# Eight blocks of tokens in a new order: the two-tile block of layer 1 second instead of last, with new scheduling priorities

## The chip, the cores and the metric

The kernel runs on one core of a Trainium2 chip. The metric is the device time of one execution in microseconds (us), lower is better. TensorE (PE) multiplies matrices, VectorE (DVE), ScalarE (ACT) and GpSimd (POOL) work elementwise, SyncE (SP) issues the transfers.

## The reference

Three stages follow each other. First an mLSTM over 768 steps, 4 batches and 8 heads of size 40, with a recurrent state `C`, a normalizer `n` and a running maximum `m`:

```
for t in range(S):
    m_new = np.maximum(f_gate[:, :, t] + m, i_gate[:, :, t])
    f_stab = np.exp(f_gate[:, :, t] + m - m_new)
    i_stab = np.exp(i_gate[:, :, t] - m_new)
    C = f_stab[:, :, None, None] * C + i_stab[:, :, None, None] * np.einsum('bhd,bhe->bhde', vt, kt)
    n = f_stab[:, :, None] * n + i_stab[:, :, None] * kt
    ...
    y[:, :, t] = o * h_tilde / denom
```

Its result, 3072 tokens of 320 features, goes through two layers of 320 to 2048 to 320. The first has a leaky ReLU, the second `h * cos(h)`:

```
h = x @ w_in
g = np.maximum(0.01 * h, h)      # layer 2: g = h * np.cos(h)
return g @ w_out
```

## The kernel before

The tokens are cut into 24 tiles of 128 (two batches by 64 steps). A tile of attention (called tile c below) is made in chunked form: scores of 64 by 64 per head (`a_scores`), weighted by products of the gates (`a_scan`, `a_weigh`), then `a_out` multiplies them with the values, reads the state of the tile two before and makes the state's increment. VectorE adds and normalizes (`a_ys`, `a_norm`, `a_scale`, `a_gate`), TensorE transposes the result (`x_turn`, L469), and ScalarE and VectorE split it into a high and a low part (`x_hi`, `x_lo`, L481 and L482). Two tiles of each 64 steps are independent; the next two need their states.

Each layer works in blocks of tiles (`BLOCKS1`, `BLOCKS2`), and each block in 16 slots, one for each 128 columns of the hidden width. In a slot `m_in` (L705) does eight matmuls of up to 512 columns, ScalarE and VectorE apply the nonlinearity and split its result (`m_leak` and `m_lo`; in layer 2 `m_turns`, `m_arg`, `m_cos`, `m_mul`, `m_hi`, `m_lo`), and `m_out` (L773) does three matmuls for each tile into banks that hold over all 16 slots. A block of layer 1 can start when the attention of all its tiles is done. A hidden tile of layer 1 has two banks of PSUM (ring `h`), but in the last block of layer 1 and in layer 2 there are four, since the attention's banks (`p`, `tr`) are then free.

The weights come as 64-bit floats. For each slot a weight is decoded (`w_bits` L386, `w_tail` L390, `w_sign` L394, `w_round` L398 on POOL, `w_mask` L402) and split into high and low (`w_hi` L201 or L199, `w_lo` L417). The sixteen weights of layer 1 are decoded beside the first tiles and block 0. Those of layer 2 are decoded during layer 1, stored, loaded again and split in the last block of layer 1, each when the weight in its buffer is no longer used. While TensorE has nothing else, `g_busy` (L251) keeps it at filler matmuls until the first slots.

What sets the order is a planner, `Schedule.run`, which runs when the kernel is built. Every piece of work is a task with a priority (a due time), a duration, the tasks that it needs, and the buffers that it takes and frees. The planner steps through a simulated time: of the tasks that could start soonest on an engine (within `SLACK`) it takes the one with the lowest priority number, and the instructions of each engine are issued in that order. On the chip each engine keeps this order and waits for semaphores. The due time of an attention tile is `t_need[c]`, that of a slot `t_slot`:

```
t_need[c] = t - ATT_LEAD - (m - 1 - j) * ATT_GAP if n else t - (m - 1 - j) * ATT_STEP
...
slot = max(slot, SLOT0)
...
p = t_slot[0, 0, i] - DEC_LEAD
plan_split(0, i, p + OFF["w_hi"], plan_decode(0, i, p))
```

and each step of a tile or slot stands at its due time minus or plus an offset in `OFF`. `T_START` is the planned time of the first slot, `SLOT0` the least planned length of a slot in block 0, `OUT_LAG` how far behind its slot an `m_out` stands.

Of the kernel before, what the change touches and what calls it, by code (L numbers as in the profile page):

```python
# [43 lines left out]
F32_MAX = float(np.finfo(np.float32).max)  # L44
STEEP = math.atanh(0.5) / (1.06 * 2.0 ** -15)

BLOCKS1 = [4, 3, 3, 3, 3, 3, 3, 2]
BLOCKS2 = [3] * 8
LAT = 0.204
SLACK = 0.05  # L50
SLOW = 50.0
T_START = 19.114
ATT_LEAD = 11.227
BACKLOG = 0.465
HORIZON = 180.0
ATT_GAP = 17.089
ATT_STEP = 8.185
OUT_LAG = 8.751
SLOT0 = 5.678
DEC_LEAD = 5.605  # L60
BUSY = [-1.11, 44.0, 0.7, -11.9]
SPREAD = 4
TURNS = [(0, 2), (2, 4), (4, 8), (8, 12)]
GATES_AT = 40.379
TURN_LEAD = 27.165
W2 = {0: -2.233, 1: -16.869}
OFF = {
    "fb": 109.16, "kvo": 6.159, "qk": 17.437, "vext": -8.48, "scan": 108.588, "kt": 17.196, "s": 16.51, "weigh": 96.927, "out": 14.378,
    "sig": 19.521, "ys": 107.91, "norm": -34.5, "scale": 120.878, "gate": 83.183, "state": 89.383, "decay": 60.278, "tr": 76.529,
    "x2": 15.514, "l_a": -93.128, "l_g": -74.411, "l_cos": 40.715, "l_mul": 46.316, "l_gh": 57.895,  # L70
    "l_gl": 97.565, "w_round": -23.988, "w_mask": 40.019, "w_hi": -83.534, "w_lo": 94.398, "w_load": 20.018,
}

ORDER = [(s, p) for s in range(NS) for p in range(B // 2)]
# [6 lines left out]
class Schedule:  # L81
# [13 lines left out]
    def run(self):  # L95
# [3 lines left out]
        while todo:  # L99
# [3 lines left out]
            for n, t in enumerate(todo):  # L103
                prio, _, key, alts, fn, args, deps, take, free, after, tab, size = t
                if prio > limit:
                    break
                ready = max(after, dma - BACKLOG) if size else after
                for d in deps:
# [19 lines left out]
            for eng, cs in cands.items():  # L128
                first = min(c[0] for c in cs)
                c = min((c for c in cs if c[0] <= first + SLACK), key=lambda c: c[1:])  # L130
                if len(todo[c[2]][3]) > 1:
# [4 lines left out]
                    if c[0] + c[3] > end + 1e-9:  # L136
# [3 lines left out]
                        first = min(x[0] for x in rest)  # L140
                        c = min((x for x in rest if x[0] <= first + SLACK), key=lambda x: x[1:])
                if best is None or (c[0], c[1]) < best[0]:
# [26 lines left out]
def mlstm_moe(ctx, tc, qk, kvo, ig, fg, w1, w2, const, out):  # L169
# [24 lines left out]
    sch = Schedule()  # L194
# [13 lines left out]
    def dvp(n):  # L208
        return ("DVE", 0.065 + n * 0.00105)
# [122 lines left out]
    def plan_gates():  # L332
# [11 lines left out]
        for j in range(2):  # L344
            sch.add(("eye", j), -4, ("POOL", 1.2, "port"), g_eye, j, deps=["cst"])
        for c0, c1, pr in ((0, 2, -3.0), (2, NS, GATES_AT)):
            n = (c1 - c0) * T
# [8 lines left out]
        for c0, c1 in TURNS:  # L356
            pr = {0: -3.0, 2: GATES_AT}.get(c0, t_need[BLOCKS1[0]] - TURN_LEAD)
            ring = "acc" if c0 < 4 else "tr"
# [6 lines left out]
            sch.add(("col", c0), pr + 0.7, dvp(48 * (c1 - c0)), g_input, c0, c1, deps=[("turn", c0)], free=[(ring, ("pt", c0))])  # L365
        sch.add("sf", GATES_AT + 0.5, SP, g_store, 2, NS, deps=[("cut", 2)], free=[("st", "f")], **dma(10 * T, BH))

# [72 lines left out]
    def plan_weights():  # L440
        for i in range(NF):
            p = t_slot[0, 0, i] - DEC_LEAD
            plan_split(0, i, p + OFF["w_hi"], plan_decode(0, i, p))
        n = len(BLOCKS1) - 1
        t0, t1 = t_slot[0, 2, 0] + W2[0], t_slot[0, n, 0] - W2[1]
        for i in range(NF):
# [46 lines left out]
    state = [cp.tile([P, 2 * HD, E1], F32, name=f"state{p}") for p in range(B // 2)]  # L493
# [69 lines left out]
    def po_ring(c):  # L563
        return "acc" if c < BLOCKS1[0] else "tr"

# [75 lines left out]
    def plan_attention(n, c, j, m):  # L641
        s, p = ORDER[c]
        e = t_need[c]
        last, k = s == NS - 1, (0, c)
        c0 = max(c for c, _ in TURNS if c <= s)
        for hh in range(2):
            sch.add(("qk", c, hh), e - OFF["qk"] + 0.1 * hh, SP, a_qk, c, hh, take=[] if hh else [("raw", c, 1)],
                    deps=[("qk", c, 0)] if hh else [], **dma(8 * P, DP))
        sch.add(("kvo", c), e - OFF["kvo"], SP, a_kvo, c, take=[("kvo", c, 2)], **dma(KV))
        if c < SPREAD:  # L650
            sch.add(("fb", c), e - OFF["scan"] - 2, ("PE", 1.0), a_spread, c, deps=[("cut", 0), "cst"],
                    take=[("acc", ("fp", c), 1), ("fb", c, 1)], free=[("st", "f")])
        else:
            for r in range(2):
                sch.add(("fb", c, r), e - OFF["fb"] + 0.1 * r, SP, a_fb, c, r, deps=[("fb", c, 0) if r else "sf"],
                        take=[] if r else [("fb", c, 1)], **dma(H * T, T))
        sch.add(("scan", c), e - OFF["scan"], ("DVE", 1.13) if c < SPREAD else ("DVE", 1.13, "port"), a_scan, c,
                deps=([("fb", c)] if c < SPREAD else [("fb", c, 0), ("fb", c, 1)]) + [("eye", 0), ("eye", 1)],
                free=[("acc", ("fp", c))] if c < SPREAD else [])
        sch.add(("vext", c), e - OFF["vext"], [pool(H * E1), dve(H * E1)], a_vext, c, deps=[("kvo", c), ("col", c0)])  # L660
        kt = []
        if not last:
            kt = [("kt", c)]
            sch.add(("kt", c), e - OFF["kt"], [pool(DM), dve(DM)], a_kt, c, deps=[("kvo", c), ("scan", c)])
        sch.add(("s", c), e - OFF["s"], ("PE", 0.62), a_scores, c, deps=[("qk", c, 0), ("qk", c, 1), ("scan", c), "clear"] + kt,
                take=[("p", (c, 0), (s > 0) + (not last)), ("p", (c, 1), (s > 0) + (not last))])
        sch.add(("weigh", c), e - OFF["weigh"], dvp(4 * P), a_weigh, c, deps=[("s", c), ("scan", c)] + kt)
        sch.add(("sig", c), e - OFF["sig"], ("ACT", 0.36), a_sig, c, deps=[("kvo", c), ("exp", 2, "f"), ("exp", 2, "i")], table="sig")
        sch.add(("out", c), e - OFF["out"], ("PE", 1.05 + (0.45 if s else 0) + (0.27 if not last else 0)), a_out, c,
                deps=[("weigh", c), ("vext", c)] + ([("state", c - 2)] if s else []) + kt  # L670
                + ([("col", TURNS[-1][0])] if c == BLOCKS1[0] else []),
                take=[(po_ring(c), ("po", c), 1)], free=[("fb", c), ("raw", c), ("kvo", c)])
        if s:
            sch.add(("ys", c), e - OFF["ys"], ("DVE", 0.82), a_ys, c, deps=[("out", c)], free=[("p", (c, 0)), ("p", (c, 1))])
        sch.add(("norm", c), e - OFF["norm"], ("DVE", 0.55), a_norm, c, deps=[("ys", c) if s else ("out", c)], take=[("d", c, 1)])
        sch.add(("scale", c), e - OFF["scale"], [pool(DM), dve(DM)], a_scale, c, deps=[("norm", c), ("sig", c)], free=[("d", c)])
        sch.add(("gate", c), e - OFF["gate"], dvp(DM), a_gate, c, deps=[("scale", c)], take=[("x", k, 1)],
                free=[(po_ring(c), ("po", c)), ("kvo", c)])
        if not last:
            if s:  # L680
                sch.add(("decay", c), t_need[c - 2] - OFF["decay"], [pool(H * E1), dve(H * E1)], a_decay, c, deps=[("state", c - 2), ("col", c0)],
                        take=[("tmp", c, 1)])
            sch.add(("state", c), e - OFF["state"], dvp(H * E1) if s else [("ACT", 0.35), dvp(H * E1)], a_state, c,
                    deps=[("out", c)] + ([("decay", c)] if s else []), free=[("p", (c, 0)), ("p", (c, 1))] + ([("tmp", c)] if s else []))
        plan_x(0, n, c, j, e - OFF["tr"], ("gate", c), ax, "x", m)
# [4 lines left out]
    def h_ring(l, n, i):  # L690
        return ("h", "h", "p", "tr")[i % 4] if l or n == len(BLOCKS1) - 1 else "h"

# [104 lines left out]
    def plan_layer(l, n, c0, m):  # L797
        N = m * P
        blocks = (BLOCKS1, BLOCKS2)[l]
        for i in range(NF):  # L800
# [24 lines left out]
            if l == 0 and last:  # L825
                free.append(("w", (0, i)))
            sch.add(("mo", k), p + OUT_LAG, ("PE", 3 * min(m, 3) * pe(1, DM)[1] + 6 * max(m - 3, 0) * pe(1, DM // 2)[1]), m_out, l, n, m, i, deps=[("gl", k)] + ([("mo", (l, n, i - 1))] if i else []),
                    take=take, free=free)
        for j in range(m):
            p = t_slot[l, n, NF - 1] + OUT_LAG + 1 + 0.3 * j  # L830
            sch.add(("ev", l, n, j), p, act(DM, True), m_evac, l, n, j, deps=[("mo", (l, n, NF - 1))],
# [8 lines left out]
    t_slot, t_need = {}, {}  # L840
    t, c = T_START, 0
    for l, blocks in enumerate((BLOCKS1, BLOCKS2)):
        c = 0
        for n, m in enumerate(blocks):
            slot = pe(8, m * P)[1] + pe(3 * m, DM)[1]
            if l == 0:
                for j in range(m):
                    t_need[c] = t - ATT_LEAD - (m - 1 - j) * ATT_GAP if n else t - (m - 1 - j) * ATT_STEP
                    c += 1
                slot += (2.8 * blocks[n + 1] / NF if n + 1 < len(blocks) else 0)  # L850
            if l == 0 and n == 0:
                slot = max(slot, SLOT0)
            for i in range(NF):
# [4 lines left out]
    c = 0  # L858
# [5 lines left out]
    c = 0  # L864
# [59 lines left out]
```

## Time and profile before

| | us |
|---|---|
| median of 3 runs | 839.64 (837.85 to 840.19) |
| the profiled execution | 839.06 |
| its span, first to last instruction | 837.3 |
| TensorE busy | 816.1 |
| VectorE busy | 593.2 |
| ScalarE busy | 421.3 |
| POOL busy | 123.9 |

The span is the stretch that the trace covers; the execution has 1.76 us outside it. Busy time of TensorE includes matmuls that overlap in its pipeline, so it says little by itself: where it follows matmul upon matmul, the distance between the starts of equal groups is its pace.

### The profile page before, as it was taken

The page shows a single profiled execution, that of the slowest core. Times are in us where ns is not written, and L with a number is a line of the kernel's source. Part 1 is how long each engine was busy: PE and PEld are TensorE (multiplying, and loading weights), DVE is VectorE, ACT ScalarE, POOL GpSimd, SP SyncE. Part 2 cuts the span into 40 slices and gives each one's busy share as a digit, 9 for nine tenths or more (in the row PEclk, how much of TensorE's full clock was granted, in tenths as well). Part 3 has the DMA queues.
Part 4 walks back from the last instruction along what each step waited for, and adds up shares of the span by engine and source line. Part 5 has one row for each costly group of instructions (what it writes and reads, how often), then busy time and mean ns, then how long its engine had stood idle before and what let it go on. Part 6 is the DMA issues. An engine that isn't in the chain of part 4 may idle for free.

```text
span 837.3 us, 19224 instructions
## 1 busy us (share of the span) xinstructions
PE 816.1 (97%) x7782; PEld 780.0 (93%) x7792; DVE 593.2 (71%) x1243; ACT 421.3 (50%) x898; POOL 123.9 (15%) x102
## 2 busy tenths in 40 slices
PE   8889999999999999999999999999989999999998
PEld 5658889999999999999999999999989999999998
DVE  7899987565655655654436987878787786868685
ACT  3366543443354443444345655556555666565654
POOL 3334320000011100010000012020110202030300
PEclk7689999999999999999999999999999999999999
DMA  9464554435344353432324400000010000000000
GB/s 234 161 211 146 159 145 130 115 126 167 121 151 131 127 166 111 151 99 78 110 96 136 136 9 17 32 17 32 17 32 16 33 14 27 17 25 17 1 25 25
DMA packets 29977, 74.56 MB, mean 89 GB/s; under 512 B 4352, under 2 KB 13696, under 8 KB 29888
## 3 DMA queue, kind: packets, MB, share of 16 engines
q1 hardware_dynamic: 29888, 73.33, 28.1%
q8 instruction: 61, 1.00, 0.5%
q14 instruction: 28, 0.23, 0.1%
HBM read 59.60 MB, written 13.71 MB: 88 GB/s over the span
## 4 chain that ended last, share of the span: by engine, by line
PE 82%; DVE 12%; ACT 3%; issue 2%; POOL 0%; DMA 0%; DVEq 0%; SPq 0%; ACTq 0%
PE acc L773 36%; PE ph L705 32%; PE pair L705 4%; DVE r L730 2%; PE po L583 2%; PE pair L554 2%; DVE r L731 2%; PE tr L469 2%; PE pair L575 2%; DVE t L727 1%; ACT r L735 1%; DVE g L741 1%; PE busy L251 1%; PE pair L591 1%; DVE wf L402 1%
## 5 line engine op out<-in xcount | busy, mean ns | idle before, releaser
L705 PE MATMUL ph<-xt,w 128*128 128x384 f32 (+2 forms) x1760 | 347.0, 341 | 3.3 <-DVE xt L482 2.5
L773 PE MATMUL acc<-w,gh 128*128 128x320 f32 x1568 | 346.9, 309 | 0.0
L705 PEld LDWEIGHTS ph<-xt,w 128*128 128x128 f32 x1760 | 299.3, 189 | 11.6 <-PE acc L773 4.3
L773 PEld LDWEIGHTS acc<-w,gh 128*128 128x128 f32 x1568 | 264.2, 188 | 2.2
L773 PE MATMUL acc<-w,gl 128*128 128x320 f32 (+1 forms) x784 | 239.0, 308 | 0.0
L713 ACT ACTIVATE gh<-ph 128x384 fp32r<-128x384 f32 (+2 forms) x124 | 61.3, 494 | 208.0 <-PE ph L705 175.9
L773 PEld LDWEIGHTS acc<-w,gl 128*128 128x128 f32 x784 | 146.1, 188 | 0.3 <-DVE gl L753 0.2
L753 DVE TENSOR_TENSOR gl<-ph,gh 128x384 fp32r<-128x384 f32 (+2 forms) x124 | 69.2, 558 | 99.6 <-ACT ph L714 99.3
L735 ACT ACTIVATE r<-r,hpi 128x384 f32<-128x384 f32 x128 | 79.1, 618 | 84.8 <-DVE r L731 84.3
L398 POOL TENSOR_TENSOR wf<-wf,raw 128x704 int32<-128x704 int32 x32 | 59.2, 1850 | 326.1 <-DVE wf L386 197.3
L753 POOL TENSOR_TENSOR gl<-g,gh 128x384 fp32r<-128x384 f32 x51 | 52.0, 1020 | 314.3 <-DVE r L731 173.4
L199 ACT CAST gh<-g 128x384 fp32r<-128x384 f32 x128 | 65.3, 510 | 37.6 <-PE acc L773 33.7
L741 DVE TENSOR_TENSOR g<-ph,r 128x384 f32<-128x384 f32 x96 | 53.3, 556 | 33.2 <-ACT r L735 31.4
L714 ACT ACTIVATE ph<-ph 128x384 f32<-128x384 f32 (+2 forms) x124 | 60.8, 491 | 0.0
L727 DVE TENSOR_SCALAR t<-t 128x384 f32<-128x384 f32 x128 | 45.9, 358 | 16.7 <-ACT t L721 16.4
L730 DVE SCALAR_TENSOR_TENSOR r<-t,ph 128x384 f32<-128x384 f32 x96 | 53.2, 554 | 3.3
L705 PE MATMUL pair<-xt,w 128*128 128x384 f32 (+1 forms) x288 | 54.6, 332 | 0.0
L721 ACT ACTIVATE t<-ph 128x384 f32<-128x384 f32 x96 | 46.0, 481 | 15.9 <-PE ph L705 13.7
L731 DVE TENSOR_SCALAR r<-r 128x384 f32<-128x384 f32 x128 | 50.5, 395 | 4.4
L705 PEld LDWEIGHTS pair<-xt,w 128*128 128x128 f32 x288 | 47.9, 188 | 0.0
L753 DVE TENSOR_TENSOR gl<-g,gh 128x384 fp32r<-128x384 f32 x77 | 42.4, 551 | 1.5 <-ACT gh L199 1.4
L199 ACT CAST xt<-tr 128x256 fp32r<-128x256 f32 x96 | 25.1, 316 | 20.7 <-PE tr L469 20.4
(97 smaller groups left out, 686.9 us busy)
## 6 DMA issues: line engine op xcount, KB each, us to landing
raw<-w SPq DMA_DIRECT2D x32, 704.0 KB, 4.4
kvo<-kvo SPq DMA_DIRECT2D x24, 484.0 KB, 4.0
raw<-qk SPq DMA_DIRECT2D x48, 192.0 KB, 3.8
w2d<-wf SPq DMA_DIRECT2D x16, 352.0 KB, 2.4
wf<-w2d SPq DMA_DIRECT2D x16, 352.0 KB, 3.4
fb<-sfd SPq DMA_DIRECT2D x40, 128.0 KB, 3.4
x2d<-o SPq DMA_DIRECT2D x24, 160.0 KB, 1.9
x<-x2d SPq DMA_DIRECT2D x24, 160.0 KB, 2.2
```

The lines of the kernel that those rows point to most:

```text
L199: nc.scalar.copy(dst, src)
L398: nc.gpsimd.tensor_tensor(f, f, wraw.pop((l, i))[:, :, 0], ALU.add)
L705: nc.tensor.matmul(ph[:, :N], w[:, a:a + P], x[:, b, :N], start=k == 0, stop=k == 7)
L713: nc.scalar.activation(t["gh"][:, :N], h, AF.Prelu, alpha=0.01)
L714: nc.scalar.activation(h, h, AF.Prelu, alpha=0.01)
L727: nc.vector.tensor_scalar(a, a, MAGIC, -MAGIC, ALU.add, ALU.add)
L730: nc.vector.scalar_tensor_tensor(r, a, -TWO_PI, t["h"][:, :N], ALU.mult, ALU.add)
L731: nc.vector.tensor_scalar(r, r, -4.712388, 1.5707959, ALU.max, ALU.min)
L735: nc.scalar.activation(r, r, AF.Sin, bias=hpi)
L741: nc.vector.tensor_tensor(t["g"][:, :N], t["h"][:, :N], t["r"][:, :N], ALU.mult)
L753: on[eng].tensor_tensor(t["gl"][:, :N], t["g"][:, :N], t["gh"][:, :N].bitcast(F32), ALU.subtract)
L773: nc.tensor.matmul(po, a[:, s], w[:, b, e], start=i == 0 and k == 0 and j < 3, stop=i == NF - 1 and k == 2, skip_group_check=True,)
```

## The change

The two-tile block of layer 1 moves from the eighth place to the second. All planning constants and offsets get new values, and the planner counts more TensorE time for the scores and the outputs of a tile of attention. The instructions of the kernel and their numbers stay; what changes is which tiles share a block, and the order on each engine.

```diff
-BLOCKS1 = [4, 3, 3, 3, 3, 3, 3, 2]
+BLOCKS1 = [4, 2, 3, 3, 3, 3, 3, 3]
 BLOCKS2 = [3] * 8
 LAT = 0.204
-SLACK = 0.05
+SLACK = 0.102
 SLOW = 50.0
-T_START = 19.114
-ATT_LEAD = 11.227
-BACKLOG = 0.465
+T_START = 6.671
+ATT_LEAD = 18.353
+BACKLOG = 0.444
 HORIZON = 180.0
-ATT_GAP = 17.089
-ATT_STEP = 8.185
-OUT_LAG = 8.751
-SLOT0 = 5.678
-DEC_LEAD = 5.605
+ATT_GAP = 8.413
+ATT_STEP = 6.704
+OUT_LAG = 5.212
+SLOT0 = 7.205
+DEC_LEAD = -1.022
 BUSY = [-1.11, 44.0, 0.7, -11.9]
...
-GATES_AT = 40.379
-TURN_LEAD = 27.165
-W2 = {0: -2.233, 1: -16.869}
+GATES_AT = 44.01
+TURN_LEAD = 12.964
+W2 = {0: -18.069, 1: -4.784}
 OFF = {
-    "fb": 109.16, "kvo": 6.159, "qk": 17.437, "vext": -8.48, "scan": 108.588, "kt": 17.196, "s": 16.51, "weigh": 96.927, "out": 14.378,
-    "sig": 19.521, "ys": 107.91, "norm": -34.5, "scale": 120.878, "gate": 83.183, "state": 89.383, "decay": 60.278, "tr": 76.529,
-    "x2": 15.514, "l_a": -93.128, "l_g": -74.411, "l_cos": 40.715, "l_mul": 46.316, "l_gh": 57.895,
-    "l_gl": 97.565, "w_round": -23.988, "w_mask": 40.019, "w_hi": -83.534, "w_lo": 94.398, "w_load": 20.018,
+    "fb": 145.408, "kvo": 13.121, "qk": 9.661, "vext": -6.732, "scan": 112.461, "kt": 69.051, "s": 31.059, "weigh": 89.589, "out": 4.41,
+    "sig": 55.041, "ys": 101.5, "norm": -48.054, "scale": 99.824, "gate": 93.916, "state": 63.081, "decay": 81.563, "tr": 117.151,
+    "x2": 11.561, "l_a": -53.555, "l_g": -95.78, "l_cos": 59.96, "l_mul": 49.468, "l_gh": 47.829,
+    "l_gl": 93.073, "w_round": -8.79, "w_mask": 47.775, "w_hi": -132.008, "w_lo": 108.694, "w_load": 24.902,
 }
...
-        sch.add(("s", c), e - OFF["s"], ("PE", 0.62), a_scores, c, ...
+        sch.add(("s", c), e - OFF["s"], ("PE", 0.72), a_scores, c, ...
...
-        sch.add(("out", c), e - OFF["out"], ("PE", 1.05 + (0.45 if s else 0) + (0.27 if not last else 0)), a_out, c,
+        sch.add(("out", c), e - OFF["out"], ("PE", 1.3 + (0.45 if s else 0) + (0.27 if not last else 0)), a_out, c,
```

## Rows read from the trace of the kernel before

**Rows 1.** Busy time of the engines by stretch, with TensorE's granted clock and DMA share.

```profile
core 0: us, PE busy (x) PEld busy (x) DVE busy (x) ACT busy (x) POOL busy (x), PEclk, DMA share, GB/s
0.00:20.00 20.00, 16.68 (x236) 10.70 (x240) 16.08 (x33) 7.04 (x11) 6.75 (x12) 0.81 0.91 236
20.00:40.00 20.00, 16.76 (x364) 13.46 (x368) 16.05 (x41) 6.62 (x13) 6.73 (x5) 0.67 0.51 176
...
53.74:95.09 41.35, 40.14 (x332) 34.45 (x331) 39.95 (x52) 24.73 (x40) 17.40 (x9) 0.96 0.56 177
...
277.28:330.13 52.85, 52.85 (x667) 51.05 (x666) 31.19 (x66) 22.00 (x50) 6.68 (x4) 1.00 0.44 138
...
470.34:532.09 61.75, 58.65 (x363) 57.01 (x362) 50.85 (x111) 37.19 (x80) 9.28 (x9) 1.00 0.10 34
532.09:576.71 44.62, 44.45 (x282) 44.17 (x282) 34.66 (x80) 27.04 (x58) 7.11 (x7) 1.00 0.07 23
576.71:623.53 46.82, 44.67 (x281) 44.11 (x282) 36.43 (x80) 26.54 (x58) 7.12 (x7) 1.00 0.07 22
```

**Rows 2.** TensorE in order of time (start, length): consecutive m_in groups of three block sizes.

```profile
73.65 2.05 PE L705 MATMUL ph<-xt,w 128*128 128x512 f32 x8
...
77.49 2.05 PE L705 MATMUL ph<-xt,w 128*128 128x512 f32 x8
...
404.84 1.55 PE L705 MATMUL ph<-xt,w 128*128 128x384 f32 x8
...
407.54 1.55 PE L705 MATMUL ph<-xt,w 128*128 128x384 f32 x8
...
451.47 1.10 PE L705 MATMUL pair<-xt,w 128*128 128x256 f32 x8
...
453.29 1.10 PE L705 MATMUL ph<-xt,w 128*128 128x256 f32 x8
```

**Rows 3.** TensorE in order of time: the first slots, with idle time before.

```profile
52.14 0.52 PE L469 MATMUL tr<-ident,x 128*128 128x128 f32 x3 [3.78 <-DVE x L638]
...
53.74 3.66 PE L705 MATMUL ph<-xt,w 128*128 128x512 f32 x8
...
57.91 2.11 PE L705 MATMUL ph<-xt,w 128*128 128x512 f32 x8
```

**Rows 4.** VectorE in order of time: weight work just before the first slot.

```profile
42.30 0.88 DVE L402 SCALAR_TENSOR_TENSOR wf<-wf,sg 128x704 f32<-128x704 f32 x1
...
45.97 2.55 DVE L417 TENSOR_TENSOR w<-wf,w 128x704 fp32r<-128x704 f32 x2
...
51.07 0.52 DVE L386 TENSOR_SCALAR wf<-raw 128x704 int32<-128x704 int32 x1
...
51.91 1.90 DVE L386 TENSOR_SCALAR wf<-raw 128x704 int32<-128x704 int32 x1
```

**Rows 5.** VectorE and TensorE in order of time: the fourteenth weight and its slot.

```profile
105.19 0.89 DVE L417 TENSOR_TENSOR w<-wf,w 128x704 fp32r<-128x704 f32 x1
...
112.78 2.12 PE L705 MATMUL ph<-xt,w 128*128 128x512 f32 x8
```

**Rows 6.** Groups of instructions, 277.28 to 330.13 us: count, busy us, mean ns, idle before.

```profile
L753 DVE TENSOR_TENSOR gl<-ph,gh 128x384 fp32r<-128x384 f32 x16 | 8.9, 556 | 13.3 <-ACT ph L714 13.3
```

**Rows 7.** TensorE in order of time: the longest wait in block 0.

```profile
95.09 0.52 PE L469 MATMUL tr<-ident,x 128*128 128x128 f32 x3 [0.93 <-DVE x L638]
```

**Rows 8.** VectorE in order of time: the scaling step of two consecutive tiles.

```profile
120.72 0.49 DVE L633 TENSOR_TENSOR kvo<-kvo,d 128x320 f32<-128x320 f32 x1
...
129.88 0.48 DVE L633 TENSOR_TENSOR kvo<-kvo,d 128x320 f32<-128x320 f32 x1
```

**Rows 9.** Waits of TensorE: us in total, times, longest.

```profile
PE ph L705 <- DVE xt L482: 2.5, 7, 0.7
PE tr L469 <- DVE g L741: 2.2, 2, 1.5
```

**Rows 10.** The chain that ended last, then VectorE in order of time: the end.

```profile
824.57 9.24 PE acc L773 x63
...
830.28 0.56 DVE L753 TENSOR_TENSOR gl<-g,gh 128x384 fp32r<-128x384 f32 x1 [0.71 <-ACT gh L199]
```

**Rows 11.** VectorE in order of time: a mask in block 0.

```profile
79.54 2.42 DVE L402 SCALAR_TENSOR_TENSOR wf<-wf,sg 128x704 f32<-128x704 f32 x1
```

More of the change, by code (lines that the diff above doesn't have):

```diff
@@ L664, in plan_attention @@
             sch.add(("kt", c), e - OFF["kt"], [pool(DM), dve(DM)], a_kt, c, deps=[("kvo", c), ("scan", c)])
-        sch.add(("s", c), e - OFF["s"], ("PE", 0.62), a_scores, c, deps=[("qk", c, 0), ("qk", c, 1), ("scan", c), "clear"] + kt,
+        sch.add(("s", c), e - OFF["s"], ("PE", 0.72), a_scores, c, deps=[("qk", c, 0), ("qk", c, 1), ("scan", c), "clear"] + kt,
                 take=[("p", (c, 0), (s > 0) + (not last)), ("p", (c, 1), (s > 0) + (not last))])
```

## The prediction

> **What bounds the kernel now.** I read the stretches first [rows 1]. TensorE is busy without a gap from about 95 us to 470 us and nearly so after it, and its clock stands at 1.00 there, the upper level of 2.4 GHz. Before 95 us it is VectorE that is full: 16.08 of 20 us, 16.05 of 20 us, then 39.95 of 41.35 us. The reader is to see two regimes: a start paced by VectorE, and a long part paced by the matmuls.
>
> Next the steady pace of a slot in TensorE's order of time [rows 2]: from one group of eight m_in matmuls to the next it is 3.84 us in the block of four tiles (77.49 - 73.65), 2.70 us in a block of three (407.54 - 404.84), 1.82 us in the block of two (453.29 - 451.47). Sixteen slots of each block, both layers: 16 x (3.84 + 1.82 + 14 x 2.70) = 695.4 us. An attention tile adds, from a block of layer 1 in the middle, (52.85 - 16 x 2.70) / 3 = 3.2 us [rows 1, 2]; 20 tiles come after the first slot: 64 us. The 24 transposed tiles of layer 2 add (44.62 - 43.2) / 3 = 0.47 us each, 11 us. The first slot stands at 53.74 us [rows 3], and behind the last matmul (824.57 + 9.24 = 833.8) [rows 10] come 3.5 us. Together 695.4 + 64 + 11 + 53.7 + 3.5 = 827.6 of a span of 837.3. So about 10 us of the span are waits and slow first slots after the start, and the start itself is 53.74 us. No reorder can touch more than these two.
>
> The profiled execution took 839.06 us, 1.76 more than its span and 0.58 under the median of 839.64. I sum against 839.06.
>
> **The change, part by part.**
>
> *What runs.* No instruction is added or removed: the same eight blocks, so the 695.4 us stay. The block sizes move attention only: block 1 now asks for two tiles beside the slots of block 0, not three, and block 2's three tiles must be made beside a block of 16 x 1.82 = 29.1 us plus 3 x 3.2, 38.7 us, not 52.85.
>
> *The larger TensorE cost of a tile* (0.62 to 0.72 and 1.05 to 1.30, 0.35 us a tile) enters only the planner's clock. It costs nothing by itself: where TensorE is full, its order holds whatever the plan thought. If that cover goes, a tile planned 0.35 us late costs 0.35 us once, below what I can resolve.
>
> *The start.* The first slot needs all four tiles of block 0. In the last 12 us before it VectorE does seven instructions of weight work, 0.88 + 0.52 + 0.88 + 2.55 (two) + 0.52 + 1.90 = 7.25 us by their rows, between the steps of tile 3 [rows 4]. That work is not urgent: the fourteenth weight, the one with the least time to spare, is ready at 105.19 + 0.89 = 106.1 and used at 112.78 [rows 5], 6.7 us early. The change also takes VectorE work out of the next stretch. A tile of attention costs VectorE at most (31.19 - 8.9) / 3 = 7.4 us in the steady block, where 8.9 us are the sixteen leak remainders and the rest still holds some weight work [rows 1, 6], and one tile fewer is asked of block 0, with tile 4's due time later. So weights may run later and tile 3 earlier. The upper bound is all of 7.25 us and the 3.78 us that TensorE waits for tile 3's x [rows 3], about 11 us; the lower bound is nothing, or a loss (below). In the new numbers tile 3's kt stands 62 ahead of zero and no longer behind it, its vext at 13.4 and not 27.6, and the weights step 7.2 apart and not 5.68, so fewer outrank it; its norm stays low (54.7, 53.6), and weight remainders gain rank. Mixed, so I take about half of 7.25: -4 us, first slot near 50 us.
>
> *TensorE's clock at the start.* The granted clock is 0.81 and 0.67 in the first two stretches [rows 1], a mix of both levels, and the first eight m_in matmuls, right after a wait, take 3.66 us where the next eight take 2.11 [rows 3]: 1.6 us lost once. I leave it as it is. The Trainium skill, page TensorE: Matmul & The Clock Gate, section What's actually happening, says the engine's default is half rate and sustained work releases it; an earlier slot behind a wait would then run at half rate again. The trace agrees for the first eight. By that rule the sum would lose one or two more such groups, which is a rival below.
>
> *Waits in block 0.* TensorE waits 0.93 us at 95.09 for tile 4's x [rows 7]. With tile 4 due later these go: -1 us, bounds 0 and -1.
>
> *Block 1 of two tiles.* VectorE: at most 3 x 7.4 + 8.9 = 31 of 38.7 us, the remainders taken at a three-tile block's price. The banks of a tile's outputs are single; two tiles follow each other there in 9.2 us at best (129.88 - 120.72) [rows 8], and 12.9 us each are at hand. I take +1 us; bounds 0 and +6 (turn of 15 us).
>
> *End of layer 1.* From 470.34 to 532.09 TensorE is idle 3.1 of 61.75 us with VectorE at 50.85, where a usual stretch of layer 2 idles 0.17 of 44.62 [rows 1]. The second layer's weights can be split only when a slot of the last block has freed its buffer, and these 16 slots pass in 1.82 us each. With three tiles they pass in 2.70. I take half of 3.1: -1.5 us, bounds 0 and -3.1.
>
> *Layer 2.* One block took 46.82 us instead of 44.62 [rows 1], because the transposes and the m_in groups that use the transposes' bank waited for VectorE [rows 9]. New offsets may move that either way; I take 0, bounds -2.2 and +13 (six more such blocks).
>
> *The tail.* At the end seven m_outs are queued behind the last m_in, 63 matmuls, 9.24 us, and hide the last slot's chain, which ends at 830.28 + 0.56 = 830.84 [rows 10]. The new OUT_LAG (5.2 for 8.75) lets m_outs go earlier, so fewer are left: the chain of at most 830.84 - 824.57 = 6.3 us asks for five slots of 9 matmuls as cover. +1 us, bounds 0 and +2.5.
>
> *Loads.* The 16 DMA engines are 0.91 busy in the first 20 us [rows 1], and tile 3's kvo is now asked for earlier, its qk later. No TensorE wait in the trace ends with a transfer after that, so 0; without that cover a load late by a few us would fall into the start. POOL, with 17.40 of 41.35 us busy beside block 0 [rows 1], has room for the steps that are moved past its queue.
>
> *Sum.* 839.06 - 4 - 1 + 1 - 1.5 + 0 + 1 = 834.6 us.
>
> **The rivals.**
>
> - *The start does not move.* The serial chain of four tiles sets it, and weight work only fills its gaps. For it: the 3.78 us wait and VectorE's idle time before 40 us [rows 1, 3]. Then -0.5 is left: 838.6 us, no change.
> - *The start moves but into half rate.* Two more groups of eight at the lower clock, 1.6 to 1.8 us each by [rows 3]: 834.6 + 3.6 = 838.2 us, no change. This is the page's rule named above. Against it: the filler matmuls are untouched.
> - *Block 1 starves.* A tile needs 15 us and not 12.9: 834.6 + 5 = 839.6 us, no change. Against it: 9.2 us was reached.
> - *Weights go before tile 3* (slower). Their remainders now rank ahead of the norm up to weight 9 and not 5. Place: VectorE before the first slot. Two weights more there, one at the short rows (0.52 + 0.88 + 0.89 = 2.3) and one at the long ones (1.90 + 2.42 + 1.28 = 5.6) [rows 4, 5, 11]: first slot 7.9 us later, 839.06 + 7.9 - 0.5 = 846.5 us. It decides from 3.6 us on. Against it: a mask ranks behind tile 3's norm in the new numbers, and only four weights can be in flight.
> - *Layer 2 slips in most blocks* (slower). Four more blocks at +2.2: 834.6 + 8.8 = 843.4 us. For it: it happened in one; against: four blocks in a row did not.
>
> **How the numbers follow.** A measurement here can tell about 0.3%, 2.5 us, from no change: faster means under 837.1, slower over 842.2. Chances: the forecast 0.60 (831 to 837.1), start unmoved 0.15, half rate 0.03, block 1 starved 0.06, weights first 0.10, layer 2 slips 0.06. Faster 0.60, same 0.15 + 0.03 + 0.06 = 0.24, slower 0.16. The range goes from 828, where the start gives 10 us, to 841 and leaves out the two slow cases, 0.16, and a little below.
>
> **What would show it.** Right: the first 512-column m_in stands near 50 us (46 to 52), with less weight work of VectorE in the 12 us before it; no TensorE wait over 0.5 us from there to the 256-column block, which now follows; that block lasts 38 to 41 us; less than 2 us of idle at the change of layers. Wrong: the first slot at 53 or later; a TensorE wait for a tile's x inside the 256-column block; blocks of layer 2 at 46.8 us; TensorE idle between the last m_in and the last m_out.

## The result, and the profile after

The changed kernel took 832.04 us (median of 4 runs, 830.60 to 833.34) beside 839.28 us (4 runs) for the kernel before on the same chip: ratio 0.9915, 95% interval 0.9893 to 0.9937. Later, beside other kernels, it took 833.0 us (6 runs), ratio 0.9929 (0.9915 to 0.9942). The profiled execution took 832.19 us with a span of 830.4, against 839.06 and 837.3 before: 6.9 us of span are won.

Where they were won is read from ScalarE, which copies out a block's sums when its last m_out is done. Three such copies, of the end of layer 1, of the first block of layer 2 and of the last block, cut the span; the first fence is of before, the second of after (start, length):

```profile
475.79 0.74 ACT L199 COPY o<-acc 128x320 f32<-128x320 f32 x2
...
525.15 0.74 ACT L199 COPY o<-acc 128x320 f32<-128x320 f32 x2
...
832.96 1.30 ACT L199 COPY o<-acc 128x320 f32<-128x320 f32 x3 [2.71 <-PE acc L773]
```

```profile
473.43 0.75 ACT L199 COPY o<-acc 128x320 f32<-128x320 f32 x2
...
521.76 0.87 ACT L199 COPY o<-acc 128x320 f32<-128x320 f32 x2
...
826.11 1.31 ACT L199 COPY o<-acc 128x320 f32<-128x320 f32 x3 [2.71 <-PE acc L773]
```

| part | before | after | won |
|---|---|---|---|
| start and layer 1 | 475.79 | 473.43 | 2.4 |
| change of layers and first block of layer 2 | 49.36 | 48.33 | 1.0 |
| the seven other blocks of layer 2 | 307.81 | 304.35 | 3.5 |

So half of the gain is in the layer for which the prediction summed nothing. The stretches after, to be laid beside [rows 1]:

```profile
core 0: us, PE busy (x) PEld busy (x) DVE busy (x) ACT busy (x) POOL busy (x), PEclk, DMA share, GB/s
...
46.81:56.17 9.36, 7.41 (x35) 5.14 (x33) 8.43 (x11) 5.54 (x8) 4.79 (x3) 0.88 0.61 193
...
124.26:163.88 39.62, 39.62 (x544) 38.30 (x539) 27.39 (x63) 18.26 (x52) 7.17 (x6) 1.00 0.52 161
...
521.76:566.21 44.45, 44.45 (x283) 44.18 (x282) 37.37 (x86) 27.43 (x59) 1.43 (x1) 1.00 0.07 23
```

What to see: the block of two tiles, now second, lasts 39.62 us and TensorE is busy in all of it. A block of layer 2 lasts 44.45 us without a gap; before, the usual one took 44.62 and one took 46.82. GpSimd (POOL) has 1.43 us of work in such a block where it had 7.11, and VectorE has 37.37 where it had 34.66.

The first slots on TensorE, to be laid beside [rows 3]:

```profile
46.81 2.21 PE L705 MATMUL ph<-xt,w 128*128 128x512 f32 x8
48.87 1.70 PE L251 MATMUL busy<-idle 128*128 128x512 bf16 x7
51.86 0.56 PE L773 MATMUL acc<-w,gh 128*128 128x320 f32 x2 [1.29 <-ACT gh L713]
53.07 0.41 PE L773 MATMUL acc<-w,gl 128*128 128x320 f32 x1 [0.65 <-DVE gl L753]
...
56.17 2.74 PE L705 MATMUL ph<-xt,w 128*128 128x512 f32 x8
58.84 0.29 PE L322 MATMUL pt<-ident,i 32*64 32x16 f32 x4
...
63.05 0.31 PE L327 MATMUL pt<-scratch,ones 32*64 32x64 f32 x4
```

The first slot stands at 46.81 us, 6.9 earlier than 53.74. But the second stands only at 56.17, and behind it come two groups of transposes of the gates (58.84 to 60.0 and 62.09 to 63.3, in front of the third slot and behind it), 2.4 us in all, which in the kernel before ended at 27.8 and 39.6, ahead of the first slot, where VectorE sets the pace [rows 1]. The second group of m_in took 2.74 us, at a granted clock of 0.79 (56.17 to 58.90); the third took 2.13.

Of the 6.9 us of the first slot, 2.4 are left at the end of layer 1, and all that is lost is lost in block 0: from its first slot to ScalarE's first copy (133.03 before, 127.35 after) it lasts 80.5 us where it had 79.3, though one tile of attention fewer (3.2 us by the prediction's price) stands beside it.

TensorE's waits after (us in total, times, longest), of which the first lies before the first slot. In order of time none stands between 65 and 431 us, and the two for xt (0.61 at 431.35, 0.97 at 476.78) are all that is left of those of [rows 9]; the two for leak and remainder at the first m_out (1.29 and 0.65) stand in the fence above:

```profile
PE tr L469 <- DVE x L638: 2.0, 1, 2.0
PE ph L705 <- DVE xt L482: 1.6, 2, 1.0
```

The end of the chain is that of [rows 10], 6.85 us earlier:

```profile
817.72 9.25 PE acc L773 x63
```

### The profile page after: what moved, and what is told of

It reads as the page before. It is cut to its first block, busy times and chain, and to the rows that moved or that the text cites. A ratio compares the mean times of both kernels' runs of the same rounds, so it can differ in the third digit from the quotient of the medians.

```text
span 830.4 us, 19165 instructions
## 1 busy us (share of the span) xinstructions
PE 814.2 (98%) x7784; PEld 778.9 (94%) x7792; DVE 606.7 (73%) x1280; ACT 421.8 (51%) x893; POOL 94.9 (11%) x70
## 4 chain that ended last, share of the span: by engine, by line
PE 94%; DVE 2%; DMA 2%; issue 1%; ACT 1%; SPq 0%; DVEq 0%; ACTq 0%
PE acc L773 42%; PE ph L705 37%; PE pair L705 6%; PE po L583 2%; PE tr L469 2%; PE pair L554 2%; PE pair L575 2%; DMA raw<-w 1%; PE pair L591 1%; DMA kvo<-kvo 1%; DVE wf L402 0%; PE acc L583 0%; PE busy L251 0%; PE pt L322 0%; PE acc L521 0%
## 5 line engine op out<-in xcount | busy, mean ns | idle before, releaser
L735 ACT ACTIVATE r<-r,hpi 128x384 f32<-128x384 f32 x128 | 79.1, 618 | 45.7 <-DVE r L731 45.2
L398 POOL TENSOR_TENSOR wf<-wf,raw 128x704 int32<-128x704 int32 x32 | 64.2, 2008 | 246.8 <-ACT raw L390 136.1
L753 DVE TENSOR_TENSOR gl<-g,gh 128x384 fp32r<-128x384 f32 x122 | 67.1, 550 | 1.5 <-ACT gh L199 1.5
L741 DVE TENSOR_TENSOR g<-ph,r 128x384 f32<-128x384 f32 x96 | 53.5, 557 | 17.1 <-ACT r L735 15.6
L705 PE MATMUL pair<-xt,w 128*128 128x384 f32 x288 | 56.6, 339 | 0.0
L731 DVE TENSOR_SCALAR r<-r 128x384 f32<-128x384 f32 x128 | 46.0, 360 | 4.4
L753 POOL TENSOR_TENSOR gl<-g,gh 128x384 fp32r<-128x384 f32 x6 | 8.4, 1399 | 330.3 <-ACT gh L199 330.3
```

The source lines that it names most:

```text
L398: nc.gpsimd.tensor_tensor(f, f, wraw.pop((l, i))[:, :, 0], ALU.add)
L705: nc.tensor.matmul(ph[:, :N], w[:, a:a + P], x[:, b, :N], start=k == 0, stop=k == 7)
L731: nc.vector.tensor_scalar(r, r, -4.712388, 1.5707959, ALU.max, ALU.min)
L735: nc.scalar.activation(r, r, AF.Sin, bias=hpi)
L741: nc.vector.tensor_tensor(t["g"][:, :N], t["h"][:, :N], t["r"][:, :N], ALU.mult)
L753: on[eng].tensor_tensor(t["gl"][:, :N], t["g"][:, :N], t["gh"][:, :N].bitcast(F32), ALU.subtract)
```

## The experiments

Each time stands beside the kernel before, run on the same chip (medians of 839.04 to 839.12 us in all of these).

### The order of the blocks alone, and the constants alone

The kernel before with the new order:

```diff
-BLOCKS1 = [4, 3, 3, 3, 3, 3, 3, 2]
+BLOCKS1 = [4, 2, 3, 3, 3, 3, 3, 3]
```

> The kernel before with only the order of blocks changed, all constants and costs as before. Theory (the changed kernel's 7.2 us come in three parts: about 2.5 at the start, about 1 at the change of layers, about 3.4 in layer 2 from the new offsets): the blocks alone save the wait in block 0 and the change of layers, 1 to 2.5 us, so 837 to 838.5 us, with the first slot still at 53 to 54 us and one block of layer 2 or more slipping by 2.2 us. Rival, the order of blocks carries the whole gain: 832 us. Second rival, blocks without the priorities that fit them stall in the block of two: over 840 us.

849.47 us, ratio 1.0118 (1.0094 to 1.0141): over 840, as the second rival had it, but TensorE has no wait of 0.3 us in the block of two. Its trace shows where the 10 us are lost, on TensorE at the last block of three tiles and at the change of layers, with the old constants; these are the two longest waits, and three more, of 2.01, 1.37 and 0.70 us, stand between 433 and 545 us:

```profile
482.88 2.90 PE L705 MATMUL ph<-xt,w 128*128 128x384 f32 x8 [3.80 <-DVE xt L482]
...
515.09 0.55 PE L469 MATMUL tr<-ident,x 128*128 128x128 f32 x3 [3.65 <-DVE g L741]
```

The changed kernel with the old order:

```diff
-BLOCKS1 = [4, 2, 3, 3, 3, 3, 3, 3]
+BLOCKS1 = [4, 3, 3, 3, 3, 3, 3, 2]
```

> The changed kernel with the block of two tiles back in the eighth place. Theory: the first slot stays at about 47 us and layer 2 keeps its period of 44.45 us, but block 0 must make three tiles beside its slots with VectorE full, and the change of layers costs 2 to 3 us again: 834 to 837 us. Rival, the new constants carry the whole gain: 832 us. Second rival, blocks carry it: 839 us.

830.19 us, ratio 0.9896 (0.9879 to 0.9912). Whether that beats the changed kernel was asked of the latter once more:

> The changed kernel once more, unchanged, beside the next three kernels on the same chip. If the order of the blocks is worth nothing by itself, it gives 830 to 832 us, and the kernel with the old order (830.2) is no faster than it by more than the measurement tells; if the old order is truly better, it gives 832 again.

833.0 us, 0.9929 (0.9915 to 0.9942): the theory of 834 to 837 us for the old order fell to its first rival, and the old order is as good with the new constants, and by the medians 2 to 3 us better (its interval meets that of the first measurement of the changed kernel, and just misses that of the second). So the new order is not what made the kernel faster; with the old constants it costs 10 us, and the new constants bring all of the gain. In the trace of the old order, the gates' transposes stand in the hole behind the first slot instead of after it:

```profile
46.74 2.20 PE L705 MATMUL ph<-xt,w 128*128 128x512 f32 x8
...
50.06 0.31 PE L327 MATMUL pt<-scratch,ones 32*64 32x64 f32 x4
...
54.47 0.31 PE L327 MATMUL pt<-scratch,ones 32*64 32x64 f32 x4
...
55.62 2.65 PE L705 MATMUL ph<-xt,w 128*128 128x512 f32 x10
```

### What the start gave, and what holds it

The changed kernel with the gates' last transposes due earlier:

```diff
-TURN_LEAD = 12.964
+TURN_LEAD = 21.377
```

> The changed kernel with TURN_LEAD larger by one ATT_GAP (12.964 + 8.413), so that the last transposes of the gates have the due time that they have with the old order of blocks, where they stood in the hole between slots 0 and 1 and not between slots 1 and 3. Theory: of the about 2 us that the old order of blocks is faster, the 2.3 us of these transposes are the cause, so 829.5 to 830.5 us. Rival, the old order is faster for another reason (the block of two tiles itself): 831.5 to 832.5 us.

829.79 us, 0.9894 (0.9876 to 0.9911), as expected: the transposes end at 49.1 and 53.5 us, in the hole, and slot 1 follows at 54.31:

```profile
45.42 2.21 PE L705 MATMUL ph<-xt,w 128*128 128x512 f32 x8
...
48.75 0.31 PE L327 MATMUL pt<-scratch,ones 32*64 32x64 f32 x4
...
53.16 0.31 PE L327 MATMUL pt<-scratch,ones 32*64 32x64 f32 x4
...
54.31 4.03 PE L705 MATMUL ph<-xt,w 128*128 128x512 f32 x16
```

The 2 to 3 us by the medians agree with the 2.4 us that their place costs the changed kernel, but do not prove it alone: in this profile the first slot too stands 1.4 us earlier (45.42 for 46.81), and the second group has no slow start (4.03 us for two).

The changed kernel with fewer filler matmuls, which hold the bank that the second slot wants:

```diff
-BUSY = [-1.11, 44.0, 0.7, -11.9]
+BUSY = [-1.11, 38.0, 0.7, -11.9]
```

> The changed kernel with the filler matmuls planned to end at 38.0 and not 44.0. In the changed kernel the first slot stands at 46.8 us but the second at 56.2, and fillers stand between them; the fillers' tile is one of the two banks that a slot of layer 1 needs, held until the last filler. Theory: this bank is what the second slot waits for, so it moves from 56.2 to about 52 us and 3 to 5 us are gained: 827 to 829 us. Rival, VectorE and ScalarE pace these slots (the leak of slot 0 waits behind weight work), the gap stays in another form: 831 to 833 us. Second rival, without fillers the first slots run at the lower clock: over 833 us.

830.92 us, 0.9900 (0.9885 to 0.9915): 1 to 2 us, not the 3 to 5 of the theory. The first two slots now run back to back, and the first m_out stands where it stood:

```profile
46.96 4.05 PE L705 MATMUL ph<-xt,w 128*128 128x512 f32 x16
52.01 0.56 PE L773 MATMUL acc<-w,gh 128*128 128x320 f32 x2 [0.99 <-ACT gh L713]
53.22 0.42 PE L773 MATMUL acc<-w,gl 128*128 128x320 f32 x1 [0.65 <-DVE gl L753]
...
55.76 1.56 PE L705 MATMUL ph<-xt,w 128*128 128x512 f32 x3
```

The second slot did come forward, but that is not what the time hangs on, and the price that the theory of the fillers gave fell. What the m_out waits for is the leak of ScalarE, and in the changed kernel that engine stands behind casts of weights, which wait for VectorE's masks (ScalarE in order of time; with fewer fillers the same leak stands at 51.38):

```profile
49.80 0.78 ACT L199 CAST w<-wf 128x704 fp32r<-128x704 f32 x1 [0.83 <-DVE wf L402]
...
51.23 0.58 ACT L713 ACTIVATE gh<-ph 128x512 fp32r<-128x512 f32 x1
```

Slot 0 had its last matmul by 49.0 us, and its leak began at 51.23. So weights that were not yet made before the first slot are made behind it. The first m_out waits for them, and in the changed kernel the second slot stands behind that m_out in TensorE's order.

Both edits at once (fillers to 40.0):

> The changed kernel with the gates' transposes' lead at 21.377 us and the fillers ending at 40.0. If the two gains stand beside each other (transposes back ahead of the slots, first slots earlier): 828 to 829.5 us. The rival, that VectorE's work on the weights fills what the earlier start opens: 830 to 832.

830.7 us, 0.9899 (0.9887 to 0.9912): the gains do not add, as the rival said. And the fillers' edit upon the old order of blocks:

> The block of two tiles last, the new constants, and fillers planned to end at 38.0. Theory (the bank held by the fillers): 830.2 less 3 to 5 us: 825 to 827.5 us. Rival, the gap stays in another form, the more so as the gates' last transposes no longer have a hole to stand in: 829 to 831 us.

837.03 us, 0.9978 (0.9965 to 0.9991), 6.8 us more than the old order without it. TensorE now waits for weights and remainders in block 0; the first two of four such waits of over 0.5 us up to 120 us:

```profile
71.87 1.65 PE L705 MATMUL ph<-xt,w 128*128 128x512 f32 x6 [0.86 <-DVE w L417]
...
81.26 0.41 PE L773 MATMUL acc<-w,gl 128*128 128x320 f32 x1 [1.58 <-DVE gl L753]
```

Here the order of the blocks is worth something: with two tiles beside block 0 the edit gains 1 to 2 us, with three it costs 7. That agrees with the room of which the prediction spoke: in the 80 us from the first slot VectorE is busy 73.8 us with three tiles and this edit, 67.8 with two. But without the edit three tiles took 68.3 us and cost nothing, so that they leave no room is not shown by itself; the planner moved other work too. Turn lead, fillers, both, or the old order: the four kernels end at 829.8 to 830.9 us, 1 to 3 us under the changed kernel, and none is apart from the others.

### The TensorE cost of a tile in the planner

The changed kernel with the old costs:

```diff
-        sch.add(("s", c), e - OFF["s"], ("PE", 0.72), a_scores, c, ...
+        sch.add(("s", c), e - OFF["s"], ("PE", 0.62), a_scores, c, ...
...
-        sch.add(("out", c), e - OFF["out"], ("PE", 1.3 + ...
+        sch.add(("out", c), e - OFF["out"], ("PE", 1.05 + ...
```

> The changed kernel with the two TensorE costs of an attention tile taken back (0.72 to 0.62, 1.30 to 1.05 us in the planner). Theory: these numbers only move the planner's clock, the start and layer 2 keep what the other constants gave: 831 to 833.5 us. Rival, the truer cost is what keeps the order of the engines together: 835 us or more.

834.87 us, 0.9949 (0.9931 to 0.9968): 1.9 and 2.8 us over the two medians of the changed kernel, with intervals that overlap. It lies between the theory (831 to 833.5) and the rival (835 or more), and it is slower by no more than the measurement tells. Whether the costs matter stays open.

### Layer 2

The kernel before with the changed kernel's eight values for slots, and nothing else: six offsets of a slot's steps, the lead of layer 2's loads (`x2`), and `OUT_LAG`. Three of them (`l_a`, `l_g`, `OUT_LAG`) serve the slots of layer 1 too:

```diff
-OUT_LAG = 8.751
+OUT_LAG = 5.212
...
-    "x2": 15.514, "l_a": -93.128, "l_g": -74.411, "l_cos": 40.715, "l_mul": 46.316, "l_gh": 57.895,
-    "l_gl": 97.565, ...
+    "x2": 11.561, "l_a": -53.555, "l_g": -95.78, "l_cos": 59.96, "l_mul": 49.468, "l_gh": 47.829,
+    "l_gl": 93.073, ...
```

> The kernel before with only the constants of the slots from the change (the six offsets of a slot's steps, that of the second layer's loads, and OUT_LAG). Theory: layer 2 goes at 44.45 us a block with no block at 46.8, so about 3 us are saved there and the start stays: 835.5 to 837 us. Rival, the period of layer 2 comes from something else in the change (the longer last block or the new weight times): 838.5 to 840 us.

835.9 us, 0.9965 (0.9952 to 0.9978): as expected. ScalarE's copies show that all of it is behind layer 1 (the end of layer 1 stands at 475.99, 0.2 later than before, the last one 3.3 earlier); of its remainders in layer 2, 6 stand on GpSimd and 122 on VectorE, as in the changed kernel, where the kernel before has 51 and 77:

```profile
475.99 0.74 ACT L199 COPY o<-acc 128x320 f32<-128x320 f32 x2
...
829.68 1.30 ACT L199 COPY o<-acc 128x320 f32<-128x320 f32 x3 [2.71 <-PE acc L773]
```

The changed kernel without them, that is, with the old offsets and OUT_LAG (the same diff turned round):

> The changed kernel with the constants of the slots taken back to those of before (the mirror of the run before). Theory: the start stays as in the changed kernel, layer 2 goes at 44.6 us a block with one or two slips again: 834.5 to 836.5 us. Rival, slot constants do nothing: 832 us.

904.6 us, 1.0781 (1.0758 to 1.0804): a miss by 70 us. 8 of the 72 us above the changed kernel are lost by the end of layer 1 (copy at 481.21, for 473.43), the rest behind it. A block of layer 2 takes 53 us and the remainders (gl) stand on GpSimd in 116 of 128 slots; the groups of instructions show it (count, busy us, mean ns):

```profile
L753 POOL TENSOR_TENSOR gl<-g,gh 128x384 fp32r<-128x384 f32 x116 | 117.7, 1015 | 366.5 <-ACT gh L199 362.7 <-DVE t L727 1.8 <-PE pair L705 1.8
L731 DVE TENSOR_SCALAR r<-r 128x384 f32<-128x384 f32 x128 | 97.6, 762 | 4.4
```

The second row is VectorE's clamp of the argument, on the path to the slot's cosine: 762 ns on the mean, 360 in the changed kernel, where GpSimd has 6 remainders, and 395 in the kernel before, where it has 51:

```profile
L753 POOL TENSOR_TENSOR gl<-g,gh 128x384 fp32r<-128x384 f32 x51 | 52.0, 1020 | 314.3 <-DVE r L731 173.4 <-ACT gh L199 69.3 <-DVE t L727 67.8
```

```profile
L753 DVE TENSOR_TENSOR gl<-g,gh 128x384 fp32r<-128x384 f32 x122 | 67.1, 550 | 1.5 <-ACT gh L199 1.5
...
L731 DVE TENSOR_SCALAR r<-r 128x384 f32<-128x384 f32 x128 | 46.0, 360 | 4.4
L753 POOL TENSOR_TENSOR gl<-g,gh 128x384 fp32r<-128x384 f32 x6 | 8.4, 1399 | 330.3 <-ACT gh L199 330.3
```

In order of time the two stand together, in the kernel of 904.6 us:

```profile
568.39 0.99 POOL L753 TENSOR_TENSOR gl<-g,gh 128x384 fp32r<-128x384 f32 x1 [2.27 <-ACT gh L199]
568.61 0.99 DVE L731 TENSOR_SCALAR r<-r 128x384 f32<-128x384 f32 x1
569.69 0.61 ACT L735 ACTIVATE r<-r,hpi 128x384 f32<-128x384 f32 x1 [1.38 <-DVE r L731]
```

The clamp starts 0.22 us after the remainder and ends 0.22 us after it. The Trainium skill, page SBUF — State Buffer, section Who interferes with whom, says that a tensor_scalar whose operands allow a two-port mode takes the port pair that VectorE shares with GpSimd, and that the second to come is then blocked for the whole instruction of the first. The rows agree in kind: 0.99 us beside a remainder, with the end behind the remainder's, and 0.36 without one.

ScalarE's cosine (L735) waits for that clamp. Its idle time before it, first in this kernel, then in the one below with all remainders on VectorE:

```profile
L735 ACT ACTIVATE r<-r,hpi 128x384 f32<-128x384 f32 x128 | 79.0, 617 | 150.4 <-DVE r L731 150.1
```

```profile
L735 ACT ACTIVATE r<-r,hpi 128x384 f32<-128x384 f32 x128 | 79.0, 617 | 83.7 <-DVE r L731 83.7
```

The rival, that it is the remainder's own length on GpSimd (1.02 us for 0.55) that holds TensorE up, has little for it: TensorE's longest waits in the kernel of 904.6 us are for g (25.9 us in all) and xt (11.6), both VectorE's, and its waits for a remainder on GpSimd come to 0.4 us in all (those of its weight loads).

So the theory became: the remainders on GpSimd lengthen VectorE's chain, and moving them to VectorE is what layer 2 gained. Two kernels put it to the test by the same edit, one on the kernel of 904.6 us, one on the kernel before:

```diff
-                sch.add(("gl", k), p + OFF["l_gl"], [dve(N), pool(N)], m_lo, ...
+                sch.add(("gl", k), p + OFF["l_gl"], [dve(N)], m_lo, ...
```

> The changed kernel with the old offsets of layer 2's slots (904.6 us), and gl remainders on VectorE alone. If the 116 remainders on GpSimd make layer 2's blocks 53 us long, they fall back to some 44.5 and the time to 832 to 838 us. The rival, that the old offsets themselves don't fit the new costs: it stays above 880.

850.33 us, 1.0127 (1.0112 to 1.0142): the theory has 54 of the 72 us, and the rival, that it stays above 880, fell. But 18 us remain, 7 of them lost by the end of layer 1 (copy at 480.61), where three of the eight old values act and where no cause was sought.

> The kernel before with one edit: layer 2's gl remainders may go to VectorE alone, not to GpSimd. If remainders on GpSimd, which lengthen VectorE's own work beside them, cost the kernel before its waits in layer 2, it comes down by about the 3.4 us that the change won there: 835.5 to 837 us. The rival, that layer 2's gain is from the moved offsets whatever engine has the remainders: 838.5 to 839.5.

840.96 us, 1.0031 (1.0022 to 1.0041): neither held; it is slower by 1.9 us. With every remainder on VectorE and the old offsets a block takes 45.86 us, as it does in the kernel of 850.33 us; with 51 of them on GpSimd the usual block took 44.62, so there GpSimd's share was a help. TensorE waits at the same place of each block, where one block follows the other (in the kernel of 840.96 us):

```profile
617.55 0.55 PE L469 MATMUL tr<-ident,x 128*128 128x128 f32 x3 [0.28 <-DVE g L741]
617.86 1.64 PE L705 MATMUL pair<-xt,w 128*128 128x384 f32 x8
...
621.72 1.63 PE L705 MATMUL ph<-xt,w 128*128 128x384 f32 x8 [0.91 <-DVE xt L482]
```

The same place in the changed kernel:

```profile
614.11 0.49 PE L469 MATMUL tr<-ident,x 128*128 128x128 f32 x3
614.35 1.63 PE L705 MATMUL pair<-xt,w 128*128 128x384 f32 x8
...
617.29 1.63 PE L705 MATMUL ph<-xt,w 128*128 128x384 f32 x8
```

The transposes of a tile want a bank that a slot frees by g, and the m_in behind them waits until VectorE has copied their result (xt). With the new offsets g and xt come in time, with the old ones they are late by 0.3 and 0.9 us. So the engine of the remainders is one part, which costs much when nearly all are on GpSimd; the other is the order that the offsets give to the steps at this turn, and it takes both to reach 44.45 us. Which of the eight values sets the turn right, and why the new constants with the old offsets send 116 remainders to GpSimd, was not tried.

## Why the prediction was right, and where its steps were not

It said 834.6 us, against 832.04. The mechanism that it named, an earlier start and an unbroken layer 1, holds in direction. But the order of the blocks, from which it drew the waits in block 0 and the change of layers, is not what made the kernel faster, and half of the gain came where its sum had 0. The sum is nearer than its terms, and that is in part luck: the gain forecast was too large by 1.6 us for start and layer 1 and by 0.5 for the change of layers, and against that stood the tail, whose loss of 1 us did not come, and the 3.5 us of layer 2.

**The start, -4 us, and waits in block 0, -1.** Weight work of VectorE was in fact moved from ahead of the first slot: in the last 12 us it has four instructions of it, 0.52 + 0.51 + 0.47 + 1.50 = 3.0 us, and a fifth, of 0.88, begins 0.28 us before the slot, where it had seven, 7.25 us [rows 4]; the first and the last of the four, on VectorE in order of time:

```profile
35.14 0.52 DVE L386 TENSOR_SCALAR wf<-raw 128x704 int32<-128x704 int32 x1
...
45.11 1.50 DVE L386 TENSOR_SCALAR wf<-raw 128x704 int32<-128x704 int32 x1
```

The first slot moved by 6.9 us and not 4, and the wait for tile 4's x [rows 7] is gone. But start and layer 1 together gave 2.4 us. What the sum lacked is what comes next after the first slot: the first m_out waits for work that stands behind the weight work that was put off (1.29 + 0.65 us, where the prediction's sign of being right was no wait over 0.5 us), the second slot stands behind it at 56.17, and the gates' transposes now stand in TensorE's full time, 2.4 us. The prediction priced the first slot and let all behind it move along. From the first slot to the second it is 9.36 us where the pace is 3.84 [rows 2]. Of the rival of half rate a small part came true: the first group took 2.21 us, against 3.66 before, but the second took 2.74 at a granted clock of 0.79, 0.6 more than the third.

**Block 1 of two tiles, +1 us.** It cost no wait: 39.62 us, in the 38 to 41 that were named, with TensorE busy in all of it. The rival that it starves is out.

**The change of layers, -1.5 us.** Right in kind, 1.0 us by the copies. But the order of blocks alone, which the step gave as its reason, made this place worse (waits of 3.80 and 3.65 us); it needed the new constants. With them the order does pay here: from the copy of the end of layer 1 to that of layer 2's second block it is 92.78 us in the changed kernel (473.43 to 566.21) and 93.70 in the old order (471.16 to 564.86), 0.9 us.

**Layer 2, 0 us.** This is the term that failed: 3.5 us were won there. The prediction had the waits in hand [rows 9] and the bound of -2.2, the one slip. It took the usual block's 0.17 us for granted and did not ask what would end it. By the runs, the eight values of the slots alone are worth 3.2 us, so the bound was too near as well. The slip by itself needs no new offsets: with only the order changed (849.47 us) no later block slipped either, and the seven blocks took 305.69 us (copies at 537.53 and 843.22) for 307.81. The period of 44.45 us was seen only with the new offsets.

**The tail, +1 us.** It did not come: 63 matmuls, 9.25 us, stand behind the last m_in as before.

**The larger TensorE cost, nothing.** Not refuted and not shown: without it the kernel was 1.9 to 2.8 us slower, within what the intervals allow.

Of the sum of -4.5, -4 was to come from start and layer 1 with block 1, -1.5 from the change of layers, and +1 from the tail; it was -2.4, -1.0, 0, and -3.5 in layer 2, for which 0 stood.

## What to carry to other kernels

When the first use of an engine is pulled forward, price the second and third use as well: work that was put off to get there stands right behind it, and small work that used to run for nothing ahead of the start may fall into the full stretch. A pattern that repeats in every block deserves its own line in the sum even where its wait is 0.2 us, and a step that may run on either of two engines is to be priced by what it does to the other engine's instructions, not only by its own length (51 of 128 remainders on GpSimd were a help here, 116 a loss). A reordering should be tried apart from the constants that came with it: here the order cost 10 us with the old constants, and the new constants gave everything.

## What the hardware showed

VectorE's clamp (128x384, one input in SBUF) took 0.99 us beside a remainder on GpSimd and 0.36 us without, and a chain that met one in nearly every slot (116 of 128, clamp 0.76 us on the mean) ran 53 us a block, 45.86 with the same offsets and all remainders on VectorE. A remainder of the same shape took 1.02 us on GpSimd in the kernel before, about 1.40 us in the changed kernel, where it ran but six times, and 0.55 us on VectorE.
